# Transposing q and u by the DMA crossbar instead of TensorE in a linear-attention and mixer kernel

## The chip, the cores and the metric

The kernel runs on one core of one Trainium2 chip. The metric is the device time of one execution in microseconds (us), lower is better. A time is the median of several executions, with the lowest and highest in brackets. The profiled execution's span (first to last instruction) is about 1.8 us shorter than its device time.

Engines are named as in the profile: PE is TensorE, PEld its weight loads, ACT is ScalarE, DVE is VectorE, POOL is GpSimd, and SPq is the queue of instructions of SyncE, which issues the loads. SBUF and PSUM are the two memories in which the kernel keeps its tiles; PE's results go to PSUM tiles.

I use two words of my own. A **stand** is time in which PE waits with nothing to do. **Stage n** is the stretch in which the last two products of batch n run, with the attention and the token mixing of batch n+1 slotted between them. I write qT(3), u(2) and so on for the tile of batch 3 or 2.

## The reference

Eight batches, 8 heads, 576 positions, head dimension 64 (so 512 channels), everything in float32 outside:

```python
phi = lambda t: np.where(t > 0, t, np.exp(t) - 1.0) + 1.0
q_p, k_p = phi(q), phi(k)
kv  = np.einsum('bhsd,bhse->bhde', k_p, v)
z   = np.sum(k_p, axis=2)
num = np.einsum('bhsd,bhde->bhse', q_p, kv)
den = np.einsum('bhsd,bhd->bhs', q_p, z)[..., None] + 1e-06
x   = (num / den).transpose(0, 2, 1, 3).reshape(8, 576, 512)

h  = np.maximum(x.transpose(0, 2, 1) @ w_tok1, 0.0) @ w_tok2      # token mixing, 256 hidden
u  = x + h.transpose(0, 2, 1)
h2 = np.maximum(u @ w_ch1, 0.0) @ w_ch2                            # channel mixing, 1536 hidden
return u + h2
```

Two products need an operand with channels on the partitions where the operand before has positions there: `num` and `den` need q transposed (qT), and `u @ w_ch1` needs u transposed (uT). These are the transposes in question.

## The kernel before

A batch passes through these steps: loads; phi of k and q (ACT and DVE); `kv`; transposition of q; `nd` (num and den in one product, then a division on DVE); `mm1` and `mm2` (token mixing, then u on DVE); transposition of u; `mm3` and `mm4` (channel mixing). The transposes are matmuls against an identity on PE, followed by a copy from PSUM on ACT or DVE:

```python
def qtr(n, g):                       # twice for each batch: 10 transposes and one copy
    tp = ps_sm.tile([128, 2, 8, 128], BF16, ...)
    for i in range(2):
        qtr_pair(n, 2 * g + i, tp[:, i * R1:(i + 1) * R1], None)   # 5 nc.tensor.transpose each
    nc.scalar.copy(out=qT[b][:, 2 * g:2 * g + 2]..., in_=tp[:, 0:2 * R1])

def utr(n, js):                      # 16 transposes and two copies for each batch
    ...
        nc.tensor.transpose(out=tp[:, i, r, :],
                            in_=u[b][:, r, 128 * j:128 * j + 128], identity=identity)
    ...                              # utr_tail: 4 more for each pair of batches
```

The program gives each instruction its place by slots. `big` lists the groups of the two channel products, and `fill` says behind which of them a step of the next batch comes. Each engine runs its instructions in that order:

```python
AT = {"kv0": 0, "kv1": 1, "qt0": 2, "qt1": 3, "nd00": 4, "nd01": 5, ..., "nd21": 9,
      "mm1": 11, "mm2a": 14, "mm2b": 15, "mm2t": 16, "ut": 17, "utt": 19}
for n in range(2, B):
    ...
        big = m3(n) + m4(p, [0, 1, 2, 3])
        fill = fill_of(n, AT, [10, 12], [18, 20])      # slots of phi of k and of q of batch n + 2
```

Loads go to SyncE's queue as soon as the program comes to them. `prep_k` and `prep_q` issue the loads of batch n + 2 right after the phi of batch n that frees the buffer; batch 3 is loaded ahead of stage 1.

## Time and profile before

| | before |
|---|---|
| time | 293.16 us (292.76 to 293.96, 3 runs) |
| span of the profiled run | 290.8 us |
| PE busy | 274.4 us, 94% |
| granted PE clock, mean | 0.998 |
| DVE, ACT, POOL busy | 58%, 57%, 10% |

The first part of the page gives each engine's busy time, share of the span and number of instructions. The second cuts the span in 40 slices; a digit is a tenth, and PEclk is the PE clock that was granted. These are the PE line of the first part and two lines of the second, of the kernel before:

```profile
PE 274.4 (94%) x2002; PEld 156.5 (54%) x2002; DVE 168.2 (58%) x329; ACT 164.7 (57%) x254; POOL 29.3 (10%) x52
PE   8888987978999899999999999999999999999993
PEclk9999999999999999999999999999999999999999
```

PE is busy at full clock in every slice from the second quarter on, but for the last. The prediction below shows the stages, the chain of waits and SyncE's loads.

### The profile page before, as it was taken

How to read it: one execution, taken by the hardware profiler on the slowest of the kernel's cores; microseconds unless marked ns; L12 is line 12 of the kernel's file. 1: busy time of each engine (PE TensorE's matmuls, PEld its weight loads, DVE VectorE, ACT ScalarE, POOL GpSimd, SP SyncE). 2: the span in 40 equal slices, each digit the busy share in tenths (PEclk: the TensorE clock that was granted, in tenths of full speed). 3: DMA queues.
4: the chain of work that ended last, by engine and by line, in shares of the span. 5: the costliest groups of instructions: out<-in, count | busy, mean ns of one | idle time of the engine just before them, and what ended most of it. 6: DMA issues, size and time to landing. Idle time of an engine off the chain costs nothing.

```text
span 290.8 us, 5019 instructions
## 1 busy us (share of the span) xinstructions
PE 274.4 (94%) x2002; PEld 156.5 (54%) x2002; DVE 168.2 (58%) x329; ACT 164.7 (57%) x254; POOL 29.3 (10%) x52
## 2 busy tenths in 40 slices
PE   8888987978999899999999999999999999999993
PEld 8776444543754465456565465456565464544641
DVE  5885377585657948692859517791769334530021
ACT  3663875139983676756696086658694185026400
POOL 3080030012000210010000210010001200000000
PEclk9999999999999999999999999999999999999999
DMA  6999999999996970785066710011001210011031
GB/s 204 280 139 202 300 241 211 293 283 359 278 291 207 287 206 2 212 239 184 0 169 204 261 39 0 36 69 42 2 0 38 108 36 2 36 72 38 1 108 72
DMA packets 46231, 41.84 MB, mean 144 GB/s; under 512 B 14656, under 2 KB 43200, under 8 KB 46208
## 3 DMA queue, kind: packets, MB, share of 16 engines
q1 hardware_dynamic: 39712, 30.68, 37.0%
q0 software_dynamic: 6496, 10.85, 15.8%
q8 instruction: 15, 0.25, 0.4%
q14 instruction: 8, 0.07, 0.1%
HBM read 35.85 MB, written 9.44 MB: 156 GB/s over the span
## 4 chain that ended last, share of the span: by engine, by line
PE 72%; DMA 11%; SPq 5%; ACT 4%; DVE 3%; issue 2%; POOL 1%; ACTq 0%
PE h_ps L359 28%; PE c_ps L336 22%; DMA q_raw<-in_q_dram 7%; PE a_ps L231 5%; PE h_ps L242 4%; DMA wc<-in_moe_w_ch_dram 3%; SPq L106 3%; PE nd_ps L196 3%; PE c_ps L347 3%; SPq L104 2%; PE tp L173 2%; PE tp L259 2%; PE kv_ps L163 2%; ACT e L116 2%; DMA k_raw<-in_k_dram 1%
## 5 line engine op out<-in xcount | busy, mean ns | idle before, releaser
L336 PE MATMUL c_ps<-uT,wc 128*128 128x512 bf16 x384 | 92.8, 379 | 2.4 <-ACT cr L340 1.5
L359 PE MATMUL h_ps<-wc,cr 128*128 128x512 bf16 x384 | 90.4, 379 | 0.0
L340 ACT ACTIVATE cr<-c_ps 128x512 bf16<-128x512 f32 x96 | 56.5, 599 | 47.4 <-PE c_ps L336 47.1
L359 PEld LDWEIGHTS <-cr 128*128 128x128 bf16 x384 | 36.5, 98 | 39.5
L336 PEld LDWEIGHTS <-wc 128*128 128x128 bf16 x384 | 35.4, 97 | 35.6 <-issue 3.3
L369 DVE TENSOR_TENSOR o_sb<-h_ps,u 128x512 f32<-128x512 f32 x32 | 21.8, 685 | 20.2 <-PE h_ps L359 20.1
L373 POOL DMA_DIRECT2D out_dram<-o_sb x24 | 14.4, 601 | 164.1 <-DVE o_sb L369 142.3
L209 DVE TENSOR_TENSOR x<-nd_ps,den 128x512 bf16<-128x512 f32 (+1 forms) x48 | 28.9, 603 | 1.7
L130 DVE TENSOR_SCALAR e<-e 128x1280 bf16<-128x1280 bf16 (+1 forms) x34 | 16.1, 474 | 22.0 <-ACT e L116 22.0
L206 DVE TENSOR_SCALAR den<-nd_ps 128x8 f32<-128x8 f32 (+1 forms) x48 | 7.8, 162 | 34.9 <-PE nd_ps L196 34.4
L116 ACT ACTIVATE e<-k_raw 128x1280 bf16<-128x1280 f32 x16 | 20.3, 1270 | 3.3 <-DMA k_raw<-in_k_dram 3.2
L116 ACT ACTIVATE e<-q_raw 128x1280 bf16<-128x1280 f32 (+1 forms) x18 | 20.3, 1150 | 2.8 <-DMA q_raw<-in_q_dram 2.7
L263 ACT COPY uT<-tp 128x1024 bf16<-128x1024 bf16 x7 | 7.1, 1012 | 25.0 <-PE tp L259 25.0
L248 DVE TENSOR_TENSOR u<-h_ps,x 128x1024 bf16<-128x1024 f32 x14 | 16.5, 1218 | 4.8 <-PE h_ps L242 4.8
L196 PEld LDWEIGHTS <-qT 128*128 128x128 bf16 x160 | 12.5, 98 | 11.8 <-ACT qT L187 1.2
L187 ACT COPY qT<-tp 128x1280 bf16<-128x1280 bf16 x14 | 17.2, 1231 | 1.6 <-PE tp L173 1.6
L196 PE MATMUL nd_ps<-kvbd,qT 128*128 128x130 bf16 x160 | 16.8, 221 | 0.9 <-ACT kvbd L167 0.5
L234 ACT ACTIVATE ar<-a_ps 128x512 bf16<-128x512 f32 x14 | 7.5, 592 | 15.7 <-PE a_ps L231 15.7
L122 DVE TENSOR_SCALAR y<-k_raw 128x1280 bf16<-128x1280 f32 x16 | 13.2, 823 | 3.9 <-DMA k_raw<-in_k_dram 3.7
L144 ACT CAST vs<-v_raw 128x1024 bf16<-128x1024 f32 x14 | 14.8, 1055 | 0.0
L394 PE MATMUL bank<-identity 128*128 128x128 bf16 x168 | 13.3, 247 | 1.4 <-POOL identity masks.py:199 1.4
L242 PE MATMUL h_ps<-ar,w 128*128 128x512 bf16 x56 | 14.4, 379 | 0.1
(88 smaller groups left out, 287.3 us busy)
## 6 DMA issues: line engine op xcount, KB each, us to landing
k_raw<-in_k_dram SPq DMA_DIRECT2D x16, 512.0 KB, 5.3
q_raw<-in_q_dram SPq DMA_DIRECT2D x16, 512.0 KB, 6.6
v_raw<-in_v_dram SPq DMA_DIRECT2D x16, 512.0 KB, 6.9
out_dram<-o_sb POOLq DMA_DIRECT2D x24, 256.0 KB, 2.9
wc<-in_moe_w_ch_dram POOLq DMA_DIRECT2D x8, 384.0 KB, 8.2
out_dram<-o_sb SPq DMA_DIRECT2D x8, 256.0 KB, 2.4
k_raw<-in_k_dram SPq DMA_DIRECT2D x16, 64.0 KB, 5.2
q_raw<-in_q_dram SPq DMA_DIRECT2D x16, 64.0 KB, 6.2
```

The source lines that it names most:

```text
L116: nc.scalar.activation(out=e, in_=f, func=AF.Exp)
L130: nc.vector.tensor_scalar(out=e, in0=e, scalar1=1.0, scalar2=None, op0=ALU.min)
L144: copy(out=vs[:, :, hs, 0:D].transpose([0, 2, 1, 3]), in_=raw["v", b][:, hs, 0:R])
L187: nc.scalar.copy(out=qT[b][:, 2 * g:2 * g + 2].rearrange("p j r c -> p (j r) c"), in_=tp[:, 0:2 * R1])
L196: nc.tensor.matmul(out=ps[:, i, a * 2 * D1:(a + 1) * 2 * D1], lhsT=qT[b][:, j, r, :], rhs=kvbd[b][:, j, :], start=True, stop=True)
L209: nc.vector.tensor_tensor(out=x[b][:, rs[0]:rs[0] + m, HG * D * g:HG * D * (g + 1)].rearrange("p r (h d) -> p r h d", h=HG), in0=v_[:, :, ...
L242: nc.tensor.matmul(out=ps[:, i], lhsT=w2t[:, kt, b, :] if r == R else w2v[:, kt, r], rhs=ar[b][:, kt, :], start=(kt == 0), stop=(kt == NT ...
L248: nc.vector.tensor_tensor(out=u[b][:, rs[0]:rs[0] + m], in0=ps[:, 0:m], in1=x[b][:, rs[0]:rs[0] + m], op=ALU.add)
L336: nc.tensor.matmul(out=ps, lhsT=wc1[:, kj, 128 * mc:128 * mc + 128], rhs=uT[b][:, kj].rearrange("p r c -> p (r c)"), start=(kj == 0), stop ...
L340: nc.scalar.activation(out=cr[b][:, mc, :], in_=ps, func=AF.Relu)
L359: nc.tensor.matmul(out=ps, lhsT=crt[:, kc, :] if t == 8 else cr[b][:, kc, 128 * r:128 * r + 128], rhs=wc2[:, kc, :], start=(kc == 0), stop ...
L369: nc.vector.tensor_tensor(out=o, in0=ps, in1=ut[p % 2] if t == 8 else u[b][:, r, :], op=ALU.add)
```

## The change

The intent is to take the transposes off the engine that bounds the kernel. The DMA engines can transpose a tile on its way from SBUF to SBUF (DMA_TRANSPOSE in the profile, a "crossbar transpose" in this text), and the DMA share of the later stages is low. So for batches 2 to 7 one DMA transpose makes qT, two make uT, and one for each pair makes the tail; batches 0 and 1 stay on PE. q is transposed as soon as its phi is done, which in the steady state is near the end of the stage ahead of its use. All these transposes are issued by SyncE. The loads of batches 3 and 4 are moved behind the transposes that would else wait for them. The core of the diff (left out: new layouts of qT and uT and the copies that fit them, two of the three transposing functions, and 20 half-size warm-up matmuls folded into one call):

```diff
+    def qtr_dma(n):
+        nc.sync.dma_start_transpose(out=qT[n % 2].rearrange("p r j c -> p (r j) c"),
+                                    in_=qp.rearrange("p r h d -> p (r h d)"))
 ...
     def prep_k(n, g):
         phi("k", n, HG * g, HG)
         vcast(n, g)
-        if n + 2 < B and n > 1:
+        if n + 2 < B and n > 2:
             load("k", n + 2, g)
             load("v", n + 2, g)

     def prep_q(n, g):
         phi("q", n, HG * g, HG)
-        if n + 2 < B and n > 1:
+        if g == 1:
+            qtr_dma(n)
+        if n + 2 < B and n > 2:
             load("q", n + 2, g)
 ...
-        out_ += [(f"qt{g}", lambda g=g: qtr(n, g)) for g in range(2)]
+        if n < 2:
+            out_ += [(f"qt{g}", lambda g=g: qtr(n, g)) for g in range(2)]
 ...
-                 ("ut", lambda: utr(n, [0, 1]))]
+        if n < 2:
+            out_.append(("ut", lambda: utr(n, [0, 1])))
+            ...
+        else:
+            out_ += [("uta", lambda: utr_dma(n, [0, 1])), ("utb", lambda: utr_dma(n, [2, 3]))]
 ...
-    for nm in "kvq":
-        for g in range(2):
-            load(nm, 3, g)
     big = m3(1) + m3t + m4(0, [4, 5, 6, 7, 8])
+    fill += [(s, lambda nm=nm, n=n, g=g: load(nm, n, g)) for n, s in ((3, 9), (4, 24))
+             for nm in "kvq" for g in range(2)]
 ...
-    AT = {"kv0": 0, "kv1": 1, "qt0": 2, "qt1": 3, "nd00": 4, ..., "mm1": 11, "mm2a": 14, ...}
+    AT = {"kv0": 0, "kv1": 1, "nd00": 3, "nd01": 4, ..., "mm1": 10, "mm2a": 12, ..., "uta": 12, "utb": 13, "utt": 15}
```

## The prediction

> **What bounds the kernel now.** I read the table of stretches first, cut where the chain of waits changes batch. I call "stage n" the stretch in which the last two products of batch n run while the attention and token mixing of batch n+1 are slotted between them; stages 1 to 4 start at 63.8, 102.1, 131.7 and 166.4 us. Columns: stretch, its length, then busy time with instruction count for PE, PEld, DVE, ACT, POOL, then granted clock, DMA share, GB/s.
>
> ```profile
> 63.80:102.10 38.30, 35.51 (x253) 19.33 (x252) 27.25 (x50) 28.30 (x41) 5.19 (x8) 1.00 0.96 283
> 102.10:131.70 29.60, 29.60 (x197) 16.01 (x196) 21.84 (x42) 19.88 (x30) 2.75 (x5) 1.00 0.59 170
> 131.70:166.40 34.70, 34.70 (x253) 19.59 (x252) 20.74 (x40) 21.41 (x32) 2.72 (x5) 1.00 0.52 161
> 166.40:196.00 29.60, 29.60 (x197) 15.97 (x196) 19.77 (x38) 19.87 (x30) 2.74 (x5) 1.00 0.11 34
> ```
>
> From 102 us on, PE is busy for the whole of each stage at full clock. Busy alone is not proof, since matmul records overlap, so I then read the chain of waits in order of time (start, length, what), where records do not overlap:
>
> ```profile
> 102.95 0.57 PE kv_ps L163 x10
> 103.52 0.86 PE c_ps L336 x4
> 104.38 0.57 PE kv_ps L163 x10
> 104.95 0.86 PE c_ps L336 x4
> 105.81 0.56 PE tp L173 x10
> 106.37 0.86 PE c_ps L336 x4
> 107.23 0.56 PE tp L173 x10
> ...
> 125.35 0.92 PE tp L259 x16
> ```
>
> Each piece starts where the last ended: 4 matmuls of 512 columns take 0.86 us (216 ns each), 10 transposes 0.56 us (56 ns each). From 102 to 286 us the bound is the count of columns streamed through PE; a transpose taken out there is worth its 56 ns. The other engines have slack (ACT 19.9 us of 29.6).
>
> Before 102 us it is different: in stage 1 the DMA share is 0.96 and ACT is busy 28.30 of 38.30 us. The timeline of SyncE shows it feeding loads there without pause, and those of DVE and PE when batch 2's q is ready and used:
>
> ```profile
> 69.53 0.59 SPq L104 DMA_DIRECT2D q_raw<-in_q_dram  x1
> ...
> 83.41 1.13 SPq L106 DMA_DIRECT2D q_raw<-in_q_dram  x1
> ```
>
> ```profile
> 78.07 0.83 DVE L131 TENSOR_TENSOR qp<-e,y 128x1280 bf16<-128x1280 bf16 x1
> ```
>
> ```profile
> 78.83 0.72 PE L173 MATMUL tp<-identity,qp 128*128 128x128 bf16 x10
> 81.75 0.41 PE L196 MATMUL nd_ps<-kvbd,qT 128*128 128x130 bf16 x4
> ```
>
> So q of batch 2 is complete at 78.9 us, PE transposes it at once, and its first product (nd) runs at 81.75, only 2.9 us later.
>
> **What the Trainium skill says.** "DMA: Bandwidth & Descriptors", Latency and other measured facts, gives a DMA transpose an effective 261 GB/s (350 to 400 if contiguous); the kernel before has none, so its trace cannot say. The same page, Anatomy of one DMA, puts some 2 us of fixed cost on a DMA, mostly the receipt; the trace agrees in size: a 128 KB store from SyncE landed after 2.3 us. "TensorE: Matmul & The Clock Gate", Part 1, has an idle PE fall to half clock and need some 3.4 us of work to recover; the trace agrees in part: the first 60 warm-up matmuls took 6.01 us, 100 ns each against the later 56, and the clock record falls within 2 us after the last matmul at 286.3. Its Part 4 gives about 275 ns for a PE transpose in a kernel; here the trace decides: 56 ns in a stream.
>
> **What the change saves.** For each of batches 2 to 7: 20 transposes of q (2 x 0.56 us) and 16 of u (0.9 us), 2.03 us; for each of three pairs 4 of the tail, 0.22 us. 6 x 2.03 + 3 x 0.22 = 12.8 us, 4.4% of 293.16. ACT also loses 12 copies of 1.23 us, 6 of 1.01 and 3 of 0.59 (22.6 us), DVE 6 of 0.69, PSUM some traffic; none of that is on the chain after 102 us. If all transposes were hidden: 293.2 - 12.8 = 280.4 us. The warm-up (92 matmuls for 102, 20 of them half size) shifts about 0.1 us; I leave it out. The new layouts of qT and uT leave rows of 128 contiguous elements; I count no cost.
>
> **What it adds.** Six crossbar transposes of q, 128x2560 bf16, 655 KB; twelve halves of u, 262 KB; three tails, 131 KB. Estimates from the skill's rate and fixed cost: q 2 + 655/261 = 4.5 us, say 5 with the wait for the semaphore; u 2 + 262/261 = 3 us. All are issued by SyncE, in order with the loads, so each waits for everything ahead in that queue: a load that waits for its buffer holds the transposes behind it, and they queue behind the bytes of the loads. The order of instructions in the two builds shows SyncE's sequence after the change: qT(2); loads of batch 3; k,v(5) first half; u(2) first half; k,v(5) second half; u(2) second half; all loads of batch 4; q(5) first half; qT(3); and so on. This is where I expect the gain to go.
>
> **Stage 1.** qT(2) cannot start before 78.9 us, as ACT and DVE set that time and the change does not touch them. It lands at about 84. In the new slots the first nd stands behind two groups of the 16-matmul tail (0.9 us each) that start at 77.04, so PE is there at 78.8 and stands for 5 us, long enough to lose the clock as well (1.5 us more, an estimate from 100 against 56 ns over the recovery). From there 20 us of work are left in the stage: it would end at 106, against 102.1. Then u(2): its DVE additions come after the phi of k(3) in DVE's order and finish about there (phi of one half is 0.83+0.49+0.83 us, one addition 1.22); the second u transpose is behind 1.2 MB of k,v(5), 4 us at 290 GB/s, so it lands at 109 to 112. Stage 2 starts 7 to 10 us late.
>
> **Stage 2.** Batch 4's loads are released only behind u(2), at some 104 us. 3.5 MB and the 0.6 MB of q(5), at the 283 GB/s of stage 1, take 14.5 us; with what is ahead the queue is clear at 120 to 124, and qT(3) lands at 124 to 129. PE wants it after four groups (4 x 0.86 + 2 x 0.57 = 4.6 us) of the stage, at 114 to 117: a stand of 10 to 12 us, and the clock lost again. In the kernel before, the first nd of this stage ran at 108.5; now at about 126. After it the rest of the stage is 23.2 us as before, less 0.9 + 0.2 of u transposes, plus 0.9 for the one group that now comes after the nd, plus 1.5 of clock. Stage 2 ends near 149 to 152 in place of 131.7: 17 to 20 us late.
>
> **Stages 3 to 7.** Loads are ahead now and few. Stages 3 to 6 save 2.03 us each, and 0.45 for tails, 8.6 in all. Against it: phi of q(n+2) is the work of the last slots of an even stage and ends about with it (131.18 + 0.83 before, stage end 131.7), so qT(4) and qT(6) leave at the boundary and are wanted 4.6 us later: 1 to 2 us of stand in each of stages 3 and 5, and 1 us for the second u of stage 2. I give 4 back: a net 4 to 5 us saved.
>
> **Sum.** 293.2 + 17 to 20 - 4 to 5 gives 305 to 309. I take 304, since each of my landing times is on the late side (the loads ran at 326 to 328 GB/s in some stretches of stage 1, and my slots on ACT are rough).
>
> **The rivals.**
> (a) All is hidden: 280 to 284 us. For it: PE-bound stages with DMA share 0.11 from 166 us, a batch of lead for q, and the care with which loads were moved. Against it: the wait for qT(2) in stage 1, where lead there is none, and the queue order ahead of qT(3).
> (b) The stands are real but short (transposes of 2 to 3 us, loads of batch 4 that reach the queue early): one stand of 3 us in stage 1 and one of 6 to 8 in stage 2 eat the 12.8; 289 to 295, "same".
> (c) The crossbar is far slower than I took it, for example 10 us for q and 5 for u: then the even stages lose 5 to 6 us each at the boundary as well, and the loads behind are delayed in their turn; 312 to 325.
> My case sits between (b) and (c).
>
> **Range and chances.** The gain is bounded by 12.8 us and well measured; the loss hangs on two landing times, qT(2) and above all qT(3). Even with a quick crossbar and 328 GB/s, qT(3) cannot land before 104 + 12.5 + 3 = 119.5 while PE, undelayed, would want it at 107: 12 us, the whole gain. So "faster" needs my reading of the queue order to be wrong; I give it 0.08, "same" 0.20, "slower" 0.72. Range 290 to 318.
>
> **What would show it.** Right: in the after profile the nd products have a new wait of PE for a DMA (qT from qp), 4 to 6 us in stage 1 and about 10 in stage 2, the chain of waits passes through loads of batch 4 and a transpose around 105 to 126 us, PE clock below full there, and from the fourth batch on stages shorter by 1 to 2 us than 29.6 and 34.7. The transposes' time to landing when nothing is ahead: 4.5 to 5 us for q, 3 for u. Wrong: stage 1 and 2 end at or before 102 and 132 us (then loads and transposes do not queue as I think), or a lone transposition takes over 8 us (then (c), and the later stages grow too), or PE stays busy but slower in the products that read the new layouts.

## The result, and the profile after

| | before | after |
|---|---|---|
| time, median (range), 4 runs each | 293.38 us (292.76 to 293.96) | 320.69 us (319.14 to 320.96) |
| span of the profiled run | 290.8 us | 318.8 us |
| PE busy | 274.4 us | 270.3 us |
| granted PE clock, mean | 0.998 | 0.944 |
| moved by DMA | 41.84 MB | 49.29 MB |

The changed kernel is slower: the ratio is 1.0921 (95% interval 1.0878 to 1.0963), and its results are correct. A ratio, here and below, is the mean time of a kernel's fast runs over that of the kernel before in the same rounds, so not quite the ratio of the medians.

The same three lines of the page, for the changed kernel:

```profile
PE 270.3 (85%) x1744; PEld 148.6 (47%) x1764; DVE 163.6 (51%) x323; ACT 144.6 (45%) x233; POOL 28.8 (9%) x52
PE   8888989797499270699589999899699999999994
PEclk9999999999699876599979999999979999999998
```

There are 238 fewer weight loads, as intended: 228 for the transposes and 10 for the changed warm-up. (The 258 fewer matmuls include 20 records that are missing from this trace.) But there are now holes in PE's line, and the granted clock falls in and behind the deep ones. The holes begin in the eleventh slice, at about 80 us, and the deep ones end in the twentieth, at 160 us. The busy time fell by only 4.1 us because matmuls at the lower clock take longer.

Next, the table of stretches of the changed kernel, cut at the ends of stages 1, 2 and 3. Columns: stretch, length, busy time with instruction count of PE, PEld, DVE, ACT and POOL, then granted clock, DMA share, GB/s:

```profile
63.20:112.50 49.30, 35.15 (x215) 19.15 (x215) 29.75 (x54) 25.13 (x38) 5.76 (x10) 0.89 0.71 194
112.50:160.70 48.20, 31.94 (x154) 15.43 (x155) 19.08 (x37) 16.30 (x26) 2.22 (x4) 0.82 0.80 188
160.70:194.70 34.00, 33.79 (x214) 18.31 (x218) 18.96 (x37) 18.42 (x29) 2.20 (x4) 0.96 0.71 185
```

With the other ends, read in the same way, all stages compare as follows (the late column is the end of the stage after the change less that before it; stage 1 starts at 63.8 and 63.2 us):

| stage | ends before | ends after | length before | length after | late at its end |
|---|---|---|---|---|---|
| 1 | 102.1 | 112.5 | 38.3 | 49.3 | 10.4 |
| 2 | 131.7 | 160.7 | 29.6 | 48.2 | 29.0 |
| 3 | 166.4 | 194.7 | 34.7 | 34.0 | 28.3 |
| 4 | 196.0 | 223.7 | 29.6 | 29.0 | 27.7 |
| 5 | 230.7 | 261.2 | 34.7 | 37.5 | 30.5 |
| 6 | 260.3 | 288.5 | 29.6 | 27.3 | 28.2 |
| 7 | 290.8 | 318.8 | 30.5 | 30.3 | 28.0 |

All the loss arises in stages 1 and 2. Stages 3 to 7, where the expected gain should have shown, win back only 1.0 us.

The timeline of PE in the changed kernel shows every stand for a DMA transpose. Columns: start, length, engine, line, operation, tiles, count, and in brackets the idle time before it with what ended it:

```profile
83.58 0.62 PE L200 MATMUL nd_ps<-kvbd,qT 128*128 128x130 bf16 x4 [5.12 <-DMA qT<-qp]
112.58 1.86 PE L349 MATMUL c_ps<-uT,wc 128*128 128x512 bf16 x4 [7.22 <-DMA uT<-u]
130.24 0.62 PE L200 MATMUL nd_ps<-kvbd,qT 128*128 128x130 bf16 x4 [11.40 <-DMA qT<-qp]
160.75 1.87 PE L349 MATMUL c_ps<-uT,wc 128*128 128x512 bf16 x4 [4.72 <-DMA uT<-u]
200.91 0.41 PE L200 MATMUL nd_ps<-kvbd,qT 128*128 128x130 bf16 x4 [1.50 <-DMA qT<-qp]
231.39 0.41 PE L200 MATMUL nd_ps<-kvbd,qT 128*128 128x130 bf16 x4 [2.98 <-DMA qT<-qp]
```

These are qT(2), uT(2), qT(3), uT(3), qT(5) and qT(6), and they add up to 32.9 us. What each one waited for is in SyncE's timeline (issue time, length of the issue):

```profile
78.51 3.17 SPq L191 DMA_TRANSPOSE qT<-qp  x1
...
105.11 1.33 SPq L333 DMA_TRANSPOSE uT<-u  x1
106.49 1.14 SPq L104 DMA_DIRECT2D k_raw<-in_k_dram  x1
...
121.44 1.06 SPq L106 DMA_DIRECT2D q_raw<-in_q_dram  x1
122.62 5.56 SPq L191 DMA_TRANSPOSE qT<-qp  x1
```

From 106.49 to 122.5 us SyncE issues the loads of batch 4 and half of q of batch 5 without a pause, and only then qT(3). Its input had long been there: DVE's timeline has the last step of q(3) end at 109.33.

```profile
108.51 0.82 DVE L131 TENSOR_TENSOR qp<-e,y 128x1280 bf16<-128x1280 bf16 x1
```

The chain of waits, in order of time (start, length, what), has qT(2) in stage 1 and goes on from qT(3) in stage 2; its last line below is the second half of uT(3):

```profile
78.51 5.02 DMA qT<-qp
...
122.62 7.57 DMA qT<-qp
130.19 0.05 issue
130.24 0.62 PE nd_ps L200 x4
130.85 1.71 PE c_ps L349 x4
...
152.18 8.44 DMA uT<-u
```

Two things are to be seen here. The transpose takes 7.57 us from issue to landing, behind those loads, where qT(2), with nothing ahead of it, took 5.02. And right after the stand, at 130.85, four 512-column matmuls take 1.71 us where they took 0.86 before: PE works at half clock, here for some 6 us after the stand.

I read the half clock off the chain behind each stand, as what the pieces took beyond their usual durations: about 2.4 us in stage 1, 1.5 after uT(2), 3.1 after qT(3), 1.3 after uT(3) and 1.7 after qT(6), an estimate of 10 us in all. (The clock record fits: it is 0.50 until about 88.4 us behind qT(2), and from 231.8 to 235.2, just behind qT(6).) The stage lengths then add up:

- Stage 1: stands 5.12 + 7.22, clock 2.4, less 2.03 for the transposes that left: 12.7. Measured 11.0. The kernel before had 38.30 - 35.51 = 2.8 us of idle PE of its own in this stage, some of which is gone; I did not split that.
- Stage 2: stands 11.40 + 4.72, clock 1.5 + 3.1, less 2.03 and a tail of 0.22: 18.5. Measured 18.6.
- Stages 3 to 7: stands 1.50 + 2.98, clock 1.3 + 1.7, less 4 x 2.03 + 2 x 0.22 = 8.6: a gain of 1.1. Measured 1.0.

So the saving of 12.8 us is there, and the waits for transposes and the clock take back three times as much.

### The profile page after: what moved, and what is told of

Its sections match the earlier page's. It is cut to its first block, busy times and chain, and to the rows that moved or that the text cites. A ratio compares the mean times of both kernels' runs of the same rounds, so it can differ in the third digit from the quotient of the medians.

```text
span 318.8 us, 4540 instructions
## 1 busy us (share of the span) xinstructions
PE 270.3 (85%) x1744; PEld 148.6 (47%) x1764; DVE 163.6 (51%) x323; ACT 144.6 (45%) x233; POOL 28.8 (9%) x52
## 2 busy tenths in 40 slices
DMA packets 76085, 49.29 MB, mean 155 GB/s; under 512 B 44512, under 2 KB 73056, under 8 KB 76064
## 3 DMA queue, kind: packets, MB, share of 16 engines
q1 hardware_dynamic: 69568, 38.15, 48.2%
## 4 chain that ended last, share of the span: by engine, by line
PE 51%; DMA 20%; SPq 9%; DVE 7%; ACT 6%; issue 4%; POOL 1%; ACTq 0%; DVEq 0%
PE c_ps L349 19%; PE h_ps L372 18%; DMA qT<-qp 9%; SPq L106 5%; PE a_ps L235 5%; DMA q_raw<-in_q_dram 5%; SPq L104 4%; PE nd_ps L200 3%; PE c_ps L360 3%; DMA uT<-u 3%; DMA wc<-in_moe_w_ch_dram 3%; ACT e L116 2%; PE h_ps L246 2%; DVE u L252 2%; DVE y L122 1%
## 5 line engine op out<-in xcount | busy, mean ns | idle before, releaser
L349 PE MATMUL c_ps<-uT,wc 128*128 128x512 bf16 x384 | 97.8, 396 | 14.4 <-DMA uT<-u 11.9
L372 PE MATMUL h_ps<-wc,cr 128*128 128x512 bf16 x374 | 88.6, 381 | 0.7 <-issue 0.2
L349 PEld LDWEIGHTS <-wc 128*128 128x128 bf16 x384 | 37.1, 101 | 52.6 <-issue 20.1
L372 PEld LDWEIGHTS <-cr 128*128 128x128 bf16 x384 | 37.2, 99 | 41.9 <-issue 0.6
L200 PE MATMUL nd_ps<-kvbd,qT 128*128 128x130 bf16 x160 | 18.5, 237 | 21.5 <-DMA qT<-qp 21.0
L200 PEld LDWEIGHTS <-qT 128*128 128x128 bf16 x160 | 13.8, 106 | 33.9 <-DMA qT<-qp 22.6
L252 DVE TENSOR_TENSOR u<-h_ps,x 128x1024 bf16<-128x1024 f32 x14 | 17.0, 1218 | 10.3 <-PE h_ps L246 10.3
L235 PE MATMUL a_ps<-x,w 128*128 128x512 bf16 x51 | 14.1, 379 | 0.3
L122 DVE TENSOR_SCALAR y<-q_raw 128x1280 bf16<-128x1280 f32 x16 | 13.4, 837 | 1.7 <-DMA q_raw<-in_q_dram 1.5
```

Of the source, the lines that this page charges most:

```text
L122: nc.vector.tensor_scalar(out=y, in0=f, scalar1=1.0, scalar2=None, op0=ALU.add)
L200: nc.tensor.matmul(out=ps[:, i, a * 2 * D1:(a + 1) * 2 * D1], lhsT=qT[b][:, r, j, :], rhs=kvbd[b][:, j, :], start=True, stop=True)
L235: nc.tensor.matmul(out=ps[:, mt], lhsT=w1t[:, b, ms] if r == R else w1[:, r, ms], rhs=x[b][:, r, :], start=(r == 0), stop=(r == R))
L252: nc.vector.tensor_tensor(out=u[b][:, rs[0]:rs[0] + m], in0=ps[:, 0:m], in1=x[b][:, rs[0]:rs[0] + m], op=ALU.add)
L349: nc.tensor.matmul(out=ps, lhsT=wc1[:, kj, 128 * mc:128 * mc + 128], rhs=uT[b][:, :, kj], start=(kj == 0), stop=(kj == NDM - 1))
L372: nc.tensor.matmul(out=ps, lhsT=crt[:, kc, :] if t == 8 else cr[b][:, kc, 128 * r:128 * r + 128], rhs=wc2[:, kc, :], start=(kc == 0), stop ...
```

## The experiments

My theory: PE stands for transposes that come too late, because they are issued in one queue with the loads and stand behind them or have no lead; and each stand costs half clock on top. Rivals: the new layouts make products or copies slower; the moved loads come too late for their own use; the crossbar's traffic slows everything else; the transposition itself is too slow wherever it stands.

In the diffs, cuts are marked by "...". Each kernel was correct. "Expected" is the text on record before the run.

### The layouts alone

The kernel before, with only the new layouts of qT and uT, the copies that fit them, and the changed warm-up.

```diff
-    qT = [const(f"qT{b}", [128, HP, R1, 128]) for b in range(2)]
+    qT = [const(f"qT{b}", [128, R1, HP, 128]) for b in range(2)]
 ...
-    uT = [const(f"uT{b}", [128, NDM, R, 128]) for b in range(2)]
+    uT = [const(f"uT{b}", [128, R, NDM, 128]) for b in range(2)]
```

> The kernel before with only the new layouts of qT and uT and the 92 plain warm-up matmuls; all transposes stay on TensorE, all loads where they were. My theory (the loss comes from PE standing for transposes that land late) expects no difference: ratio 1.00 within 0.5%, 293 us, mean of the uT-by-wc matmul still 379 ns. The rival that the strided reads of uT or the strided evictions slow PE, ACT or DVE expects 297 us or more, and a mean above 390 ns as in the changed kernel (396 ns).

Measured: 293.34 us, ratio 1.0011 (0.9966 to 1.0056). The products that read uT still take 379 ns in the mean. The layouts cost nothing.

### The moved loads alone

The kernel before, with only the loads of batches 3 and 4 where the change has them.

```diff
-        if n + 2 < B and n > 1:
+        if n + 2 < B and n > 2:
             load("k", n + 2, g)
 ...
+    fill += [(s, lambda nm=nm, n=n, g=g: load(nm, n, g)) for n, s in ((3, 9), (4, 24))
+             for nm in "kvq" for g in range(2)]
```

> The kernel before with only the loads of batches 3 and 4 moved to where the change has them; all transposes on TensorE. My theory expects little, since no PE input waits in the same queue: 293 to 297 us. The rival that the late loads are the harm by themselves (phi of batches 3 and 4 starves) expects 300 us or more, with ACT or DVE waiting for k_raw or q_raw in stages 1 and 2.

Measured: 293.52 us, ratio 1.003 (0.9977 to 1.0083). The later loads are still in time for their own use. In the changed kernel, where they stand behind the transposes as well, ACT and DVE wait 10.4 us for loads in the whole program, against 11.3 before, so there too they are in time.

### The change with the loads where they were

```diff
-        if n + 2 < B and n > 2:
+        if n + 2 < B and n > 1:
 ...
+    for nm in "kvq":
+        for g in range(2):
+            load(nm, 3, g)
 ...
-    fill += [(s, lambda nm=nm, n=n, g=g: load(nm, n, g)) for n, s in ((3, 9), (4, 24))
-             for nm in "kvq" for g in range(2)]
```

> The changed kernel with the loads of batches 3 and 4 put back where the kernel before has them (issued before the transposes of batch 2). My theory of queue order: qT(2) now stands behind k, v and half of q of batch 4, lands at 90 to 94 us instead of 83.6, so PE stands 11 to 15 us in stage 1 instead of 5.1; qT(3) then has little ahead and its stand of 11.4 us in stage 2 falls below 3. Sum 311 to 317 us. The rival that moving the loads was the mistake expects under 305 us.

Measured: 311.60 us (2 runs), ratio 1.0635 (1.057 to 1.07), as expected. PE's timeline has the stand for q in stage 1 now, and none for qT(3):

```profile
90.70 0.61 PE L200 MATMUL nd_ps<-kvbd,qT 128*128 128x130 bf16 x4 [11.21 <-DMA qT<-qp]
```

Moving the loads, which was meant to clear the way, made the changed kernel 9 us slower: it took 6 us off the stand in stage 1 and made one of 11 in stage 2. The stand goes where the loads go.

### Only the loads of batch 4 moved, behind qT(3)

```diff
-    fill += [(s, ...: load(nm, n, g)) for n, s in ((3, 9), (4, 24)) ...]
+    fill += [(s, ...: load(nm, n, g)) for n, s in ((3, 9),) ...]
 ...
+    fill += [(28, lambda nm=nm, g=g: load(nm, 4, g)) for nm in "kvq" for g in range(2)]
```

> The changed kernel with the loads of batch 4 issued after the transpose of q of batch 3 instead of before it. My theory of queue order: qT(3) lands at about 118 us, PE's stand for it in stage 2 falls from 11.4 us to under 2, and with the half clock that followed it (about 3 us) the kernel takes 304 to 309 us. The rival that the crossbar transposes themselves are slow and hold the queue expects the stand to stay above 8 us and 316 us or more.

Measured: 304.60 us (2 runs), ratio 1.0396 (1.0325 to 1.0467), as expected. The stand for qT(3) is gone; those for qT(2) (5.12), uT(2) (6.73), uT(3) (5.29) and qT(6) (3.00) remain. This one edit of order is worth 16 us of the 27, so the queue order ahead of qT(3) is the largest single cause.

### All loads of a batch behind its q transpose

The loads of batches 4 and up are issued only behind the q transpose that goes before them, to clear the way for u as well.

```diff
     def prep_q(n, g):
         ...
             qtr_dma(n)
-        if n + 2 < B and n > 2:
-            load("q", n + 2, g)
+            for m in ((4, 5) if n == 3 else (n + 2,)):
+                if 2 < n and m < B:
+                    for nm in "kvq":
+                        for i in range(2):
+                            load(nm, m, i)
```

> The run with the loads of batch 4 behind qT(3), and beyond it every load from batch 5 on issued after the transpose of q of the same stage, so that no load stands ahead of a transpose of u or q. My theory: the two stands of 6.7 and 5.3 us for the second half of u that are left in that run shrink, the first to 3 to 4 us (its transpose starts when PE is nearly there), the second under 1, the stand of 0.6 for qT(5) goes; the stands of 5.1 (qT(2)) and 3.0 us (qT(6)) stay, as no load causes them. 304.6 becomes 293 to 298 us. The rival that u waits for its own production or for a slow crossbar expects the two stands unchanged, 302 us or more.

Measured: 306.05 us (303.70 to 308.09), ratio 1.0461. A miss by 8 us, no better than the one before. The stand for uT(2) fell to 1.87, but qT(3) had one of 3.96: it left at 110.02, with no lead, and landed after 6.42 us. And uT(3) kept its stand:

```profile
134.98 1.05 SPq L106 DMA_DIRECT2D q_raw<-in_q_dram  x1
136.12 6.23 SPq L333 DMA_TRANSPOSE uT<-u  x2
...
147.05 1.87 PE L349 MATMUL c_ps<-uT,wc 128*128 128x512 bf16 x4 [6.29 <-DMA uT<-u]
```

u(3) was ready at 135.3, but I had put the loads of two batches together behind qT(3), and they were issued until 136.0. The transposes then landed at 146.9, where PE was at the end of the stage at 140.8. I had moved the queue again, not emptied it.

### The loads of batch 5 one batch later

To test that reading, the loads of batch 5 go behind qT(4), out of the way of u(3):

```diff
-            for m in ((4, 5) if n == 3 else (n + 2,)):
+            for m in ((4,) if n == 3 else (5, 6) if n == 4 else (n + 2,)):
```

(The removed line is that of the kernel just above.)

> The run with all loads last, but the loads of batch 5 issued after qT(4) in stage 2 instead of after qT(3) in stage 1. In that run PE stood 6.3 us at the end of stage 2 for u(3), whose transposes were issued 4.6 us before PE came but behind 3.5 MB of batch 5. If the loads ahead are the cause, the stand falls below 1.5 us; if late production of u or the crossbar is, it stays above 4. The total should fall from 306 to 297 to 303 us, unless batch 5 is then late in stage 3.

Measured: 304.31 us (301.48 to 304.86), ratio 1.0366, just outside what was expected. The stand for uT(3) is gone (0.26 us left), so the loads ahead were its cause. But qT(4), issued at 141.82 when the stage that uses it had begun at 140.81, now has one of its own:

```profile
148.86 0.41 PE L200 MATMUL nd_ps<-kvbd,qT 128*128 128x130 bf16 x4 [3.30 <-DMA qT<-qp]
```

In the changed kernel PE did not stand for qT(4): it left at 158.20, while PE stood for uT(3), and landed behind that stand. A wait taken away uncovered the next one.

### Batch 2 back on PE

As the kernel with all loads behind the transposes, but with batch 2 transposed on PE, since qT(2) has no lead at all.

```diff
-        if n < 2:
+        if n < 3:
             out_ += [(f"qt{g}", lambda g=g: qtr(n, g)) for g in range(2)]
```

> The run with all loads last, and batch 2 (which has no lead) back on TensorE with its slots and the loads of batch 3 as in the kernel before; batches 3 to 7 by DMA. My theory: the stands of stage 1 (5.1 us and the rest of the first u) go with their half clock, 2.0 us of TensorE work come back; stands of about 3 us are left for qT(3), and for qT(4) and qT(6) 1 to 3 us each: 286 to 292 us. If DMA transposes cost PE time in a way other than by stands, it stays above 293.

Measured: 298.85 us (297.73 to 300.42), ratio 1.0204 (1.0157 to 1.0251). A miss: stands for qT(3) (4.23), uT(3) (4.85) and qT(6) (2.97) remain.

### q of the even batches four groups earlier

The kernel just above, with the phi of q in even stages moved from slots 18 and 20 to 14 and 16.

```diff
-            fill = fill_of(n, AT, [10, 12], [18, 20])
+            fill = fill_of(n, AT, [10, 12], [14, 16])
```

> The run with batch 2 on TensorE, and phi of q in even stages four slots earlier (14 and 16 in place of 18 and 20), so that qT(4) and qT(6) start some 3.5 us earlier. My theory: the stands for qT(4) and qT(6) go, 2 to 4 us less than the run before it: 283 to 289 us, faster than both kernels. If the end of phi is set by ACT or DVE rather than by its slot, there is no gain over that run.

Measured: 298.78 us (296.26 to 300.54), ratio 1.0208. My theory missed and its rival held: relative to its stage qT(6) left only about 1.1 us earlier, because DVE, not the slot, set when q is ready (ACT's part came at the same place in the stage in both runs; DVE's last step for q(6) ended at 201.6, where qT(6) left), and it took 7.6 us to land. The stand stayed at 3.13.

### The transposes beside the kernel before, unused

The kernel before, which goes on transposing on PE, with the 18 transposes of q and u (not the tails) issued as well, into a tile that nobody reads (one output buffer fewer makes room).

```diff
+        if g == 1:
+            nc.sync.dma_start_transpose(out=dq, in_=qp.rearrange("p r h d -> p (r h d)"))
```

> The kernel before with TensorE transposes as they are, and besides them the six transposes of q and twelve halves of u by the DMA crossbar into a buffer that nothing reads (one output buffer less, to make room). My theory (only waiting for transposes costs) expects 292 to 295 us. The rival that crossbar traffic by itself slows loads, evictions or matmuls enough to matter expects 297 us or more.

Measured: 293.20 us, ratio 1.0021 (0.9984 to 1.0058), as expected. The DMA view of this kernel (number of transposes, median us from issue to landing):

```profile
dq<-u SPq DMA_TRANSPOSE x12, 4.9
dq<-qp SPq DMA_TRANSPOSE x6, 6.5
```

The traffic, and the time that SyncE takes to issue it, cost nothing in this kernel, where nobody waits for them. So the loss lies in the waiting, and in the clock behind it.

### PE kept busy in the stands

The changed kernel, with matmuls of no use placed ahead of the four largest stands (85, 115, 190 and 75 of them), so that the clock does not fall. Nothing can land earlier for it.

```diff
+    fill += [(13, lambda: warm(85))]
 ...
+    fill += [(29, lambda: warm(115))]
 ...
+            if n == 2:
+                fill = sorted([(3, lambda: warm(190))] + fill + [(23, lambda: warm(75))], ...)
```

> The changed kernel with meaningless matmuls put before the four instructions at which PE stands longest (85, 115, 190 and 75 of 56 ns), which keep PE at work while it waits for the same DMA. The transposes land no earlier, so stands are filled, not removed. My theory that each stand costs half clock besides its own length expects the half clock after them to vanish and 311 to 317 us in place of 320.7. The rival that the clock's fall lies inside the stands and costs nothing expects 319 us or more.

Measured: 316.55 us (313.85 to 317.50), ratio 1.079 (1.0744 to 1.0836), as expected. The slices of the clock:

```profile
PEclk9999999999999989999999999999989999999998
```

The mean granted clock rose from 0.944 to 0.986 and the time fell by 4.1 us (3.8 by the ratios), by filling alone: that part is shown to be the clock. It is less than the estimated 10 us, for reasons that the trace offers. Not all was filled: qT(6) (2.93, 1.7 us of clock in the estimate) was not among the four, and 2.50 us for uT(2) were left, behind which the chain still shows some 1.7 us of half clock. And PE, being faster after one stand, comes sooner to the next: qT(3) was issued at 121.81 against 122.62, hardly earlier, and a new stand of 2.30 us for qT(4) appeared. The filling for qT(3) also ran until 130.9, at least 0.7 us after it can have landed (no q took over 8.4). How much each accounts for was not separated.

### q alone by DMA

The changed kernel, with u on PE as before.

```diff
-        if n < 2:
+        if n < 8:
             out_.append(("ut", lambda: utr(n, [0, 1])))
```

> The changed kernel with u and its tails back on TensorE, q by DMA, loads as changed. My theory: the stands of 7.2 and 4.7 us for u go with about 3 us of half clock, 6.1 us of TensorE work come back, the stands for qT(2) and qT(3) stay at 5 and 10 to 12 us: 308 to 315 us, still slower than before. If u's share is what made the loss, it is below 300.

Measured: 317.86 us (317.59 to 319.19), ratio 1.0847 (1.0812 to 1.0882). A miss by 3 us: almost the whole loss is that of q. PE comes to qT(3) sooner and stands longer, because the loads of batch 4 are where they were: 13.99 us at 127.05, against 11.40 in the changed kernel.

### u alone by DMA, twice

The changed kernel, with q on PE as before. In my first version the slots of u moved back with those of q, but those of the batch-4 loads did not, so that the loads stood ahead of u(2); the second version has them behind.

```diff
-        if n < 2:
+        if n < 8:
             out_ += [(f"qt{g}", lambda g=g: qtr(n, g)) for g in range(2)]
 ...
-    fill += [(s, ...: load(nm, n, g)) for n, s in ((3, 9), (4, 24)) ...]
+    fill += [(s, ...: load(nm, n, g)) for n, s in ((3, 9), (4, 26)) ...]     # second version only
```

> The changed kernel with q back on TensorE in the old slots, u and tails by DMA, loads as changed: the counterpart of the run with u on TensorE. My theory: no stand for qT; stands of 4 to 7 us for u(2) and 3 to 5 us for u(3), half clock after them, 6.1 us of TensorE work saved: 297 to 305 us. If u alone is harmless, it is below 291.

Measured, first version: 305.32 us, ratio 1.0411, a miss: a stand of 16.43 us for uT(2), which I had built in.

> The run with q on TensorE, mended: there the slots that I moved put the loads of batch 4 ahead of u(2), and PE stood 16.4 us for it. Now they are behind it, as in the changed kernel. My theory: that stand falls to 2 to 4 us, one of about 2 us is left for u(3), 6.1 us of TensorE work stay saved: 289 to 295 us. If u's transposes cost PE more than their queue, it stays above 299.

Measured, second version: 295.75 us (295.35 to 295.89), ratio 1.0086 (1.0066 to 1.0107), just missed. Stands of 6.70 for uT(2) and 0.79 for uT(3) are left. Two slots of the same loads are worth almost 10 us. Against the kernel before of the same rounds q alone costs 317.86 - 292.73 = 25.1 us and u alone 295.75 - 293.13 = 2.6, together 27.7, against the 27.3 of the whole change. That this adds up so well is in part luck: the stand for qT(3) changed its length, and with the loads of batch 4 in their slot of the changed kernel u alone cost 12.6.

### Only the transposes that have slack

Loads stay where the kernel before has them. Only u of batches 4 to 7 and q of batches 5 and 7 go by DMA, where the time between production and use is long. The table `AT_ODD` (`nd` at slot 8) is in the program already but not used: it holds for q of even batches by DMA, which only the next version has.

```diff
+    Q_DMA, U_DMA = (5, 7), (4, 5, 6, 7)
 ...
-        if g == 1:
+        if g == 1 and n in Q_DMA:
             qtr_dma(n)
 ...
+    AT_ODD = {"kv0": 0, "kv1": 1, "nd00": 8, "nd01": 9, ..., "mm1": 15, "mm2a": 17, ..., "uta": 17, "utb": 18}
+        at = AT_PE if n + 1 not in Q_DMA else AT_ODD if b else AT
```

> A version that uses the crossbar only where the traces show slack: u of batches 4 to 7, q of batches 5 and 7 (whose phi ends well before an odd stage does), tails of the last two pairs; batches 2 and 3, q of 4 and 6, and all loads as in the kernel before. My theory: no PE stand for a DMA over 1 us, TensorE work less by 4 x 0.90 + 2 x 1.13 + 2 x 0.22 = 6.3 us: 286 to 289 us. If transposes beside loads or stores cost more than their stands, 291 or more.

Measured: 287.36 us (median of six), ratio 0.9801 (0.9774 to 0.9828) over the five fast runs (286.22 to 287.64). One execution, which happened to be the profiled one, took 404.04 us. All of it but the start ran at a lower clock, which is why it is not compared:

```profile
PEclk8666666666666666666666666666666666666666
```

The same kernel was run again.

> The version with slack only once more, unchanged, as its one profile fell on a slow execution (granted clock 0.658). My theory: 286 to 289 us, ratio 0.975 to 0.985, and in a fast profile no stand of PE for a DMA over 1 us from stage 2 on.

Measured: 286.89 us (285.73 to 289.61, 6 runs), against 293.13 for the kernel before in the same rounds; ratio 0.98 (0.9759 to 0.9841). It is faster by about 2%. These are stages 2, 3 and 4 in the table of stretches of its profile:

```profile
102.30:132.00 29.70, 29.59 (x197) 16.00 (x197) 21.95 (x43) 19.88 (x30) 2.75 (x5) 1.00 0.54 166
132.00:165.80 33.80, 33.64 (x234) 18.66 (x236) 20.36 (x39) 20.40 (x31) 3.14 (x5) 1.00 0.65 170
165.80:193.10 27.30, 27.19 (x155) 13.72 (x156) 17.48 (x35) 16.28 (x26) 2.27 (x5) 1.00 0.42 100
```

Stage 2 is as in the kernel before, and so is stage 1, which ended at 102.3 us; stage 4 takes 27.30 us against 29.60; the clock is full, and no stand of PE for a DMA is left. The q transposes take 6.4 and 8.6 us to land, and nobody notices. The saving, by the prediction's durations, should be 4 x 0.9 (u) + 2 x 1.12 (q) + 2 x 0.22 (tails) = 6.3 us. Measured: 6.24 by the medians, 5.9 by the ratio, and 5.4 and 5.8 in the same way in the first round. So a transpose taken off PE is worth about the time of its columns, provided that it is not waited for.

### All q from batch 4 on, with nd later

The same with q of batches 4 and 6 by DMA as well, which have no lead in their own stage, so that `nd` at slot 8 has to give them one.

```diff
-    Q_DMA, U_DMA = (5, 7), (4, 5, 6, 7)
+    Q_DMA, U_DMA = (4, 5, 6, 7), (4, 5, 6, 7)
```

> The run with slack only, and q of batches 4 and 6 by DMA as well, with the nd products of odd stages five slots later (8 in place of 3), so that a transpose that leaves at the stage boundary has some 9 us. My theory: 6.3 + 2 x 1.13 = 8.6 us less than before, no stand over 1 us: 284 to 287 us. If the lead is still too short, stands of 2 to 3 us for qT in odd stages and 287 to 291 us.

Measured: 287.98 us (287.06 to 290.06), ratio 0.9843 (0.9808 to 0.9878). Missed: no stand for a DMA, but in stages 3 and 5 PE now waits for DVE:

```profile
146.95 0.29 PE L200 MATMUL nd_ps<-kvbd,qT 128*128 128x130 bf16 x2 [1.26 <-DVE x L213]
```

The later `nd` put its division behind the phi of the next k in DVE's order. With a second wait of 0.56 us behind it, that makes 1.8 us for each of the two stages, more than the 1.12 of the transposes taken away.

### Two attempts to mend that

First the phi behind `nd`; then `nd` at slot 6 with the phi of k at 12 and 14 in those stages.

```diff
-            fill = fill_of(n, at, [10, 12], [18, 21])
+            fill = fill_of(n, at, [14, 17], [20, 23])
```

> The run with later nd products, and in odd stages phi of k and q moved behind them (slots 14, 17, 20, 23 in place of 10, 12, 18, 21): in that run PE stood 1.26 and 0.56 us in each of stages 3 and 5 for the division of nd on VectorE, which came after phi of k in its order. My theory: these 3.6 us go and nothing takes their place: 283 to 286 us, ratio 0.965 to 0.975, below the version with slack only. If phi then ends too late for the next even stage, a stand for kp or qT there and 287 us or more.

Measured: 290.51 us over six executions (286.67 to 292.11, two of them counted as slow), ratio of the fast ones 0.9865 (0.9816 to 0.9914). A miss: DVE's wait is gone, but q of the next batch is ready later, and a stand of 2.75 us for qT(5) took its place.

```diff
-              "nd00": 8, "nd01": 9, "nd10": 10, ...
+              "nd00": 6, "nd01": 7, "nd10": 8, ...
-            fill = fill_of(n, at, [10, 12], [18, 21])
+            fill = fill_of(n, at, [12, 14] if at is AT_ODD else [10, 12], [18, 21])
```

> The run with later nd products, with nd at slots 6 to 11 and phi of k at 12 and 14 in odd stages, so that VectorE divides before it turns to phi of k, and phi of q back at 18 and 21. My theory: the 1.8 us of stand in each odd stage go, qT(4) and qT(6) have some 3 us more than in the changed kernel, qT(5) is as early as in the run with later nd: 284 to 287 us, at or below the version with slack only. If qT(6) still comes late, a stand of 1 us or more and 287 or above.

Measured: 290.31 us over six executions: three fast (286.10 to 288.73), three at 291.90 to 292.51, which count as slow. The ratio of the fast ones is 0.9799 (0.9763 to 0.9835), no better than the version with fewer transposes (and worse if the three slow ones are its own, which the record can't tell), with stands for qT(4) (1.60), qT(5) (2.17) and qT(6) (0.45). A miss in part: not below the version with slack alone, which remains the best.

## Why the prediction was wrong, point by point

The direction and the mechanism held. The size did not: 320.69 us lies above the range that ended at 318. The step that failed is the sum from stage 2 on: it gave qT(3) the time of a transpose alone, did not follow the queue ahead of the second u of stage 2, and counted the half clock for two stands where it struck behind five.

**Held: the bound and the saving.** The bound is the count of columns on PE. The version with slack alone saved 5.9 to 6.2 us in its second round where these durations give 6.3, and the ledger of the stages closes with 12.8 us for the whole change.

**Held: a crossbar transpose alone.** I estimated 4.5 to 5 us for q and 3 for half of u. qT(2), with nothing ahead, took 5.02; the quickest u took 3.1. (The 2 us of fixed cost in the estimate came from a section on DMAs that GpSimd issues; that it fits SyncE's is what these landings show.) Rival (c), a crossbar twice as slow in itself, is not the case, though beside loads q does take up to 10.3 us. The measured time lies in the range given for (c), 312 to 325: slow transposes were part of the loss, but only beside other transfers, not in themselves.

**Held: stage 1.** qT(2) landed at 83.5, not far from 84, for a stand of 5.12 where I had 5. u(2) landed at 112.5, just past the end of 109 to 112, and stage 2 began 10.4 us late where I had 7 to 10.

**Held: the place of the largest stand.** It is qT(3), behind the loads of batch 4, 11.40 us where I had 10 to 12. The queue was clear at 122.6, inside 120 to 124. The runs that moved these loads show it is the cause: 304.60 us with them behind qT(3), and a stand of 11.21 us in stage 1 with them ahead of qT(2). The Trainium skill, "DMA: Bandwidth & Descriptors", section Queues, rings and completion order, says that on each DMA engine descriptors are consumed in the order of the ring; the trace is consistent with it, though it does not prove it: 7.57 us for qT(3) behind loads against 5.02 alone. But of the 20.9 us from q(3) being ready (109.33) to its landing, the larger part, 13.3, was spent in SyncE: it did not issue qT(3) before 122.62.

**Failed: the sum for stage 2 and after.** My sum was 305 to 309, 307 in the middle; it is short by 13.7, and three terms account for it:

- *"qT(3) lands at 124 to 129", the first nd "at about 126".* Measured 130.24, 4.2 us later: behind the loads the transpose took 7.57 us rather than 5, and it left at 122.62, some 1.6 us later than 126 less 5.
- *"After it the rest of the stage is 23.2 us", with corrections 24.5.* Measured 160.75 - 130.24 = 30.5, 6.0 us more. A stand of 4.72 us for uT(3), for which I gave "1 us for the second u of stage 2", is most of it: its second half was issued at 152.18 behind the loads of k and v of batch 6 and took 8.44 us to land (what the output stores beside it added was not separated). I followed the queue ahead of qT(3) and did not follow it ahead of the next u. Where loads ahead of it (those of batch 5, in two of the runs) were taken away, the stand fell from 6.29 us to 0.26. The rest is the clock, 3.1 us behind qT(3) where I had 1.5.
- *"A net 4 to 5 us saved" in stages 3 to 7.* Measured 1.0, 3.5 us less. The stands there were 4.5 us, close to the "4 back" that I gave; what was missing is the half clock behind uT(3) and qT(6), 3.0 us by the estimate.

**Failed: the half clock.** I counted 1.5 us for each of two stands, 3 us. It struck behind five stands, at 1.3 to 3.1 us each, some 10 us by estimate. Filling four stands with idle work gave back 4.1 us, so at least that much is shown.

**Failed: the choice in the range.** I took 304 below my own sum, "since each of my landing times is on the late side". Only that of qT(2) was, by half a microsecond; u(2), at 112.5, and qT(3), at 130.2, landed past the late end; I had put qT(3) at the time that it takes alone.

**Two lines misread.** The clock record does not fall "within 2 us after the last matmul at 286.3": cut finely it is 1.00 until 289.5 and 0.50 from 290.0, so it fell some 3.6 us after. And SyncE feeds loads "without pause" only until 84.5; it issues none from there to 90.5. Neither decided the number.

**The rivals.** (a), all hidden, and (b), short stands, did not come about. A fourth cost that I named only as something that would prove me wrong, slower products from the new layouts, is excluded by the run with the layouts alone.

**Left open.** All transposes stayed in SyncE's queue. Issuing them all from another engine, past the loads, was not tried, nor do these runs tell what such an engine's own work would lose. Which of the causes named there kept the filled kernel from gaining more than 4.1 us was not separated either, nor why three executions of the last kernel were slow. Nor do the runs show what decides whether a stand of about 3 us costs half clock: 2.98 us did in the changed kernel (1.7 us), 3.00 and 3.13 in two other runs did not.

## What to carry to other kernels

When work goes from a busy engine to a DMA, count first the time between the producer's end and the consumer's start at each place, and move only those transfers whose slack exceeds the landing time beside other traffic (here 7 us in the middle and up to 10 for 655 KB, not the 5 of a lone one). Moving loads out of the way of one transfer puts them in the way of the next, so follow the issuing queue to the end of the program for every transfer, not only for the one that worried you. Reckon with the clock as well: behind PE's waits of 4.7 to 11.4 us the half clock cost 1.3 to 3.1 us on top, by the estimate above; waits of about 3 us cost up to 1.7 or nothing, and one of 1.50 us nothing.

## What the Trainium skill lacked or had wrong

- "DMA: Bandwidth & Descriptors", Latency and other measured facts, 261 GB/s for a DMA transpose: of the right size for a lone one (655 KB landed in 5.02 us, which is 217 GB/s after 2 us of fixed cost). It does not say what happens beside loads in the same queue: here a median of 7.2 us and up to 10.3 for q, and 3.1 to 8.4 for half of u.
- No section that I found gives the time that the issuing engine itself spends on one large transpose on trn2. A table on trn3 B0 in "DMA: Bandwidth & Descriptors" has sequencer cycles for "previous generations", but does not name trn2 or the size of its tiles. SyncE took 2.9 to 3.2 us for q with little or nothing beside it and up to 5.9 beside loads, and about 1.3 us for half of u (up to 3.2 beside loads). This holds the loads behind it.
- "TensorE: Matmul & The Clock Gate", Part 4, has about 275 ns for a PE transpose in a kernel. As the duration of one that is of the right size (219 ns in the trace), but in a stream one starts every 56 ns here, and the version with slack alone gained about that (5.9 to 6.2 us against 6.3). Part 4 does not say so (Part 2 has about 56 ns between matmuls of 128 columns); who takes the 275 ns for the cost sees the change five times as good as it can be.
- The same page, Part 1, describes the half clock after an idle window, and the trace agrees (1.71 us for a group of 0.86). Its example of a kernel that waits for a DMA in each turn of a loop puts 1.67 us of throttled time, half of it lost, on each wait. It has no figure for a wait after which PE has work for long: here 1.3 to 3.1 us were lost behind stands of 4.7 to 11.4 us, by the estimate above, and nothing or up to 1.7 behind stands of about 3.
- No page was found to account for one execution at a granted clock of 0.658 on average, from early on to its end, with one core in use by this program: 404.04 us against 287.36. The notes in Part 1 of the same page on a clock stuck at a quarter and on a limit of 13/16 with three busy cores do not give this figure. Four matmuls took 1.29 us in it where they take 0.86. No run shows the cause.
